# Exponentials and gate weights written in linear order, tokens kept by (parity, group, pair)

## The chip, the cores and the metric

The kernel runs on one core of a Trainium2 chip. The metric is device time in microseconds. Two runs of the kernel before took 212.56 and 213.94 us; their median, 213.25 us, is the time to compare with. The profiled execution took 212.8 us, and its span from the first to the last instruction is 211.1 us; all times within the profile count from the start of that span.

The engines are named as the profile names them: PE is TensorE (matmuls), PEld its weight loads, DVE is VectorE, ACT is ScalarE, POOL is GpSimd, SP is SyncE, which here only issues transfers.

## The reference

Attention with 32 memory slots instead of keys, and after it a mixture of experts. Batch B = 8, heads H = 8, sequence S = 576, head size 64, memory slots M = 32, experts E = 8, D = F = 512.

```python
def _attn_ref(q, k, v, phi):
    a = np.exp(phi - np.max(phi, axis=2, keepdims=True))
    a = a / (np.sum(a, axis=2, keepdims=True) + 1e-09)
    k_m = np.einsum('bhsm,bhsd->bhmd', a, k)
    v_m = np.einsum('bhsm,bhsd->bhmd', a, v)
    scores = np.matmul(q, k_m.transpose(0, 1, 3, 2)) / np.sqrt(q.shape[-1])
    attn = np.exp(scores - np.max(scores, axis=-1, keepdims=True))
    attn = attn / (np.sum(attn, axis=-1, keepdims=True) + 1e-09)
    return np.matmul(attn, v_m)
# x = the result as (4608 tokens, 512)
def _moe_ref(x, w_gate, w1_dense, w2_dense, w1, w2):
    y_dense = np.maximum(x @ w1_dense, 0.0) @ w2_dense
    logits = x @ w_gate
    expert_idx = np.argmax(logits, axis=1)
    probs = softmax(logits)                      # cut
    gate_w = probs[np.arange(N), expert_idx]
    # each token: one expert e = expert_idx
    y_moe = gate_w * (np.maximum(x @ w1[e], 0.0) @ w2[e])
    return y_dense + y_moe
```

## The kernel before

The eight batches go through a software pipeline whose order of steps is written out by hand, one list for all engines. A step name and its batch stand in it, such as `s:4` (scores of batch 4), `ET0:4` (its first exponentials), `Z0:4`, `ln0:4`, `inv0:4`, `A0:4` (the normalised weights), `hd0:4` (first layer of the dense part), `yd0:4` (second layer), `he`, `ye` the same for the expert that most tokens of the batch choose, `o0:4` a store. Within one engine the instructions run in that order. The change keeps the list.

Inputs lie in SBUF with 64 groups of nine consecutive tokens: partition p of a head holds tokens 9p to 9p + 8. So the scores come out with columns (t, p), t from 0 to 8 the place in the group, p the group, first the five even t, then the four odd ones. The columns that leave the exponentials are put into token order, 9p + t, by the way they are written. Cut to what the change touches:

```python
P = 64; T = S // P                                # T = 9
NP = S // 256; NCH = 2 * NP + 1; REM = S - 256 * NP   # 2, 5, 64
cols = [slice(256 * (c // 2) + c % 2, 256 * (c // 2) + 256, 2) for c in range(2 * NP)]
cols.append(slice(S - 128, S))
rem = slice(S - REM, S)
even, odd = slice(0, P * (T - T // 2)), slice(P * (T - T // 2), S)

big = ctx.enter_context(tc.tile_pool(name="big", bufs=2, space=PSUM))   # p_q, p_kv, p_s, p_z, p_h
one = ctx.enter_context(tc.tile_pool(name="one", bufs=3, space=PSUM))   # p_vw, p_y

# s: scores of both halves of a batch, a = 0 and 1, each in one tile of "big"
for a in range(2):
    p_s = big.tile([128, 2, 512], F32, tag="big", name="p_s")
    st[b]["ps", a] = split(p_s)                   # 576 of the 1024 columns
...
# ET0, ET1: exponentials of half a
p_s = st[b].pop(("ps", a))
for u, cs in enumerate((even, odd)):
    nc.scalar.activation(
        out=st[b]["ET"][:, a].rearrange("m (p t) -> m t p", t=T)[:, u::2],
        in_=p_s[:, cs].rearrange("m (t p) -> m t p", p=P),
        func=AF.Exp, scale=escale)
...
# Z: sums over the 32 slots, by a matmul with blocks of ones; ln, inv: 1/sum = exp(-ln(sum))
# A: ET * inv, f16
# second layer, columns of tokens as lhsT
def second(b, c, HT, w2):
    p_y = one.tile([128, 512], F32, tag="one", name="p_y")
    at, n, parts = (rem, REM, 2) if c == NCH - 1 else (cols[c], 128, 1)
    ...
            nc.tensor.matmul(p_y[n * u : n * u + n, 0:w], lhsT=HT[:, ft, at],
                             rhs=w2[:, ft, w * u : w * u + w], ...)
# the gate logits use the same columns of A as lhsT
# o0, o1: 256 rows; o4: the last 64 rows in two halves
nc.sync.dma_start(
    out=out[S * b + 256 * c : S * b + 256 * c + 256].rearrange("(p i) d -> p (i d)", i=2),
    in_=st[b]["y"][:, 2 * D * c : 2 * D * c + 2 * D])
# wgt: the gate weights, once, at the start
o = wgt[:, i].rearrange("t e p -> t p e")
r = st[0]["wgr"][:, i].rearrange("t (p e) -> t p e", e=E)
copy(e, out=o, in_=r)                             # on ScalarE
# w1: the expert's weights; GpSimd waits for the number of the expert (choose), then issues
# w1, w2 of this batch and loads of later batches that stand behind them in its queue
```

Of the kernel before, what the change touches and what calls it, by code (L numbers as in the profile page):

```python
# [13 lines left out]
AF = mybir.ActivationFunctionType  # L14
# [53 lines left out]
def kernel(  # L68
# [13 lines left out]
    nc = tc.nc  # L82

    B, H, S, Dh = q.shape
    M = phi.shape[-1]
    D = out.shape[1]
    E = moe_w_gate.shape[1]
    F = moe_w1_dense.shape[1]
    P = 64
    T = S // P  # L90
# [3 lines left out]
    NJ = H // 2  # L94
    SC = 16.0
    escale = 1.0 / (math.sqrt(Dh) * SC)
    NP = S // 256
    NCH = 2 * NP + 1
    REM = S - 256 * NP
    cols = [slice(256 * (c // 2) + c % 2, 256 * (c // 2) + 256, 2) for c in range(2 * NP)]  # L100
    cols.append(slice(S - 128, S))
    rem = slice(S - REM, S)
    even, odd = slice(0, P * (T - T // 2)), slice(P * (T - T // 2), S)
    NKEEP = 4

    const = ctx.enter_context(tc.tile_pool(name="const", bufs=1))
# [10 lines left out]
    def copy(e, out, in_):  # L117
        (nc.scalar.copy if e == "A" else nc.vector.tensor_copy)(out=out, in_=in_)  # L118

    def split(p):  # L120
        return p.rearrange("p h c -> p (h c)")[:, 512 - even.stop : 512 - even.stop + S]

    order = ExitStack()
    order.enter_context(tc.manual_schedule())
# [22 lines left out]
    def step(*names):  # L147
        def reg(f):
            for n in names:
                steps[n] = f  # L150
            return f

        return reg

    st = [dict() for _ in range(B)]
# [15 lines left out]
    @step("Lphi")  # L171
    def _(b, i, e):
        input_tile(b, "phi")
        (nc.gpsimd if e == "P" else nc.sync).dma_start(
            out=st[b]["phi"].rearrange("p j t m -> p j (t m)"), in_=rows(phi[b])
        )
# [63 lines left out]
    def load_w1(out, e, cond=None):  # L240
        nc.gpsimd.dma_start(  # L241
            out=out, in_=moe_w1[ds(e, 1)].rearrange("o (dt p) f -> p (o dt) f", p=128), cond=cond
        )

    def load_w2(out, e, cond=None):
        nc.gpsimd.dma_start(
            out=out, in_=moe_w2[ds(e, 1)].rearrange("o (ft p) d -> p (o ft) d", p=128), cond=cond
        )
# [31 lines left out]
    @step("wgt")  # L280
    def _(b, i, e):
        wgt = wk.tile([DT, 2, E, 64], F16, tag="qT", name="wgt")
        st[0]["wgt"] = wgt
        for i in range(2):
            o = wgt[:, i].rearrange("t e p -> t p e")
            r = st[0]["wgr"][:, i].rearrange("t (p e) -> t p e", e=E)
            if e == "P":
                nc.gpsimd.tensor_copy(out=o, in_=r)
            else:
                copy(e, out=o, in_=r)  # L290
# [175 lines left out]
    @step("ET0", "ET1")  # L466
    def _(b, a, e):
        if "ET" not in st[b]:
            st[b]["ET"] = wk.tile([128, 2, S], F16, tag="ET", name="ET")
        p_s = st[b].pop(("ps", a))  # L470
        for u, cs in enumerate((even, odd)):
            nc.scalar.activation(  # L472
                out=st[b]["ET"][:, a].rearrange("m (p t) -> m t p", t=T)[:, u::2],
                in_=p_s[:, cs].rearrange("m (t p) -> m t p", p=P),
                func=AF.Exp,
                scale=escale,
            )

    @step("Z0", "Z1")
    def _(b, a, e):  # L480
# [297 lines left out]

    @step(*(f"o{c}" for c in range(NP)))
    def _(b, c, e):  # L780
        nc.sync.dma_start(
            out=out[S * b + 256 * c : S * b + 256 * c + 256].rearrange("(p i) d -> p (i d)", i=2),
            in_=st[b]["y"][:, 2 * D * c : 2 * D * c + 2 * D],
        )

    @step(f"o{NCH - 1}")
    def _(b, c, e):
        y = st[b]["y"][:, 2 * D * NP :]
        dst = out[S * b + S - REM : S * b + S]
        w = D // 2  # L790
        for u in range(2):
            eng = nc.scalar if u == 1 and e == "A" else nc.sync
            eng.dma_start(out=dst[:, w * u : w * u + w], in_=y[REM * u : REM * u + REM, 0:w])
# [30 lines left out]
    def go(text):  # L824
        for tok in text.split():
            tok, _, e = tok.partition("/")
            name, _, b = tok.partition(":")
            if name in ("kv", "kk", "vv", "kvm", "kmk", "kmv", "T", "Tk", "Tv"):
                steps[name](int(b), name, e)
                continue  # L830
            i = name if name[0] in "LFC" and name[1:2] in ("k", "v", "q") else int(name[-1]) if name[-1].isdigit() else 0
            steps[name](int(b), i, e)
# [4 lines left out]
    def others(b):  # L837
        st[b].clear()
        go(
            f"Lphi:{b}/P Lk:{b} Lv:{b} Lq:{b} e0:{b} e1:{b} z:{b} rz:{b} kv:{b} kvm:{b} T:{b} kTc:{b}/V"  # L840
            f" q0:{b} qT0:{b}/V q1:{b} qT1:{b}/V s:{b} ET0:{b} ET1:{b} Z0:{b} ln0:{b} Z1:{b} ln1:{b}"
            f" inv0:{b} inv1:{b} A0:{b} A1:{b}"
        )
        ix = sm.tile([128, NCH], F32, tag="ix", name="ix")
        nc.vector.tensor_scalar(
            out=ix,
            in0=idx[b],
            scalar1=em[:, b : b + 1],
            scalar2=100.0,
            op0=ALU.is_equal,  # L850
            op1=ALU.mult,
        )
        nc.vector.tensor_add(out=ix, in0=ix, in1=idx[b])
        y0 = wk.tile([128, 2 * NP, D], F32, tag="y", name="yx", bufs=NKEEP)
        y1 = wk.tile([128, D], F32, tag="lnz", name="yr")
        y = [y0[:, c] for c in range(2 * NP)] + [y1]
        rows_of = [
            (y0[:, 2 * c : 2 * c + 2].rearrange("p i d -> p (i d)"), S * b + 256 * c)
            for c in range(NP)
        ]  # L860
        for t, r in rows_of:
            nc.gpsimd.dma_start(
                out=t, in_=out[r : r + 256].rearrange("(p i) d -> p (i d)", i=2)
            )
        tail = out[S * b + S - REM : S * b + S]
        nc.gpsimd.dma_start(out=y1[128 - REM :], in_=tail)
        for e in range(E):
            w1e = wk.tile([128, DT, F], F16, tag="HTd", name="w1x")
            w2e = wk.tile([128, FT, D], F16, tag="qT", name="w2x")
            load_w1(w1e, e)  # L870
            load_w2(w2e, e)
            ge = sm.tile([128, NCH], F32, tag="ge", name="ge")
            nc.vector.scalar_tensor_tensor(
                out=ge,
                in0=ix,
                scalar=float(e - E),
                in1=gate[b],
                op0=ALU.is_equal,
                op1=ALU.mult,
            )  # L880
            nc.vector.tensor_scalar(
                out=ge, in0=ge, scalar1=1.0 / SC, scalar2=None, op0=ALU.mult
            )
            HTx = wk.tile([128, FT, S], F16, tag="HTe", name="HTx")
            vwx = wk.tile([128, 2, F], F16, tag="vwe", name="vwx")
            for a, p_vw in enumerate(fold(vT[b], w1e)):
                nc.vector.tensor_copy(out=vwx[:, a], in_=p_vw[:, 0:F])
            for ft in range(FT):
                nc.vector.tensor_scalar_max(
                    out=HTx[:, ft].rearrange("p (h c) -> p h c", h=2),  # L890
                    in0=hidden(vwx, st[b]["A"], ft)[:, :, 0:HC],
                    scalar1=0.0,
                )
            for c in range(NCH):
                skip = 128 - REM if c == NCH - 1 else 0
                p_y = one.tile([128, 512], F32, tag="one", name="p_y")
                for ft in range(FT):
                    nc.tensor.matmul(
                        p_y,
                        lhsT=HTx[:, ft, cols[c]],  # L900
                        rhs=w2e[:, ft],
                        start=(ft == 0),
                        stop=(ft == FT - 1),
                    )
                nc.vector.scalar_tensor_tensor(
                    out=y[c][skip:],
                    in0=p_y[skip:],
                    scalar=ge[skip:, c : c + 1],
                    in1=y[c][skip:],
                    op0=ALU.mult,  # L910
                    op1=ALU.add,
                )
        for t, r in rows_of:
            nc.gpsimd.dma_start(
                out=out[r : r + 256].rearrange("(p i) d -> p (i d)", i=2), in_=t
            )
        nc.gpsimd.dma_start(out=tail, in_=y1[128 - REM :])

    engs = (ENG.PE, ENG.DVE, ENG.Activation, ENG.Pool)
# [36 lines left out]
```

The softmax here doesn't subtract the row's maximum and nothing guards it: scores larger than these inputs give would overflow.

## Time and profile before

| | |
|---|---|
| time, median of 2 runs | 213.25 us (212.56 to 213.94) |
| span of the profiled execution | 211.1 us, 5096 instructions |
| TensorE busy | 152.9 us (72%), mean granted clock 0.913 |
| ScalarE busy | 133.6 us (63%) |
| VectorE busy | 111.7 us (53%) |
| GpSimd busy | 35.5 us (17%) |
| bytes moved by transfers | 39.34 MB, 186 GB/s over the span; HBM read 51.92 MB, written 9.44 MB |
| chain that ended last | PE 53%, ACT 26%, DMA 11% of the span |
| its largest lines | PE p_y L741 27%, ACT ET L472 20%, PE p_h L677 15%, DMA fq 7%, DMA phi 5% |

A busy share is an average over the whole span and does not tell which engine holds up which. The chain that ended last is followed back from the last instruction: at each step to what released it. The view of stages gives, for any window of time, how long each engine was busy in it, at which clock TensorE ran, and what the DMA engines did. L472 is the exponential of the scores (ET), L677 the first layer (p_h), L741 the second (p_y), L483 the sums (p_z).

The loads from HBM cast f32 to f16 on the way, apart from those of the first batch, and phi. Until about 18 us the first batch waits for its inputs; after the last matmul, at about 201.8 us, the last stores land.

### The profile page before, as it was taken

What the parts mean: (1) busy time and instruction counts of PE and PEld (TensorE: products, weight loads), DVE (VectorE), ACT (ScalarE), POOL (GpSimd) and SP (SyncE); (2) the same over time, 40 slices, a digit from 0 to 9 for tenths busy, and PEclk for the clock granted to TensorE, in tenths of its full rate; (3) what the DMA queues carried; (4) which work ended last, traced back from release to release, by engine and by line L of the source; (5) the groups of instructions that cost most, each with busy time, mean ns of one, the idle gap of its engine ahead of it and who ended that gap; (6) DMA issues with size and microseconds to landing.
All of it is one profiled execution on the core that took longest, in us unless ns stands there. A gap on an engine that the chain in (4) does not pass through costs nothing.

```text
span 211.1 us, 5096 instructions
## 1 busy us (share of the span) xinstructions
PE 152.9 (72%) x2145; PEld 85.9 (41%) x2145; DVE 111.7 (53%) x289; ACT 133.6 (63%) x184; POOL 35.5 (17%) x53
## 2 busy tenths in 40 slices
PE   0034339829995999769759993999499947999920
PEld 0033116415652565336335641554246623556410
DVE  0324147425964686648826863466509553684630
ACT  2743884397749874798786378586867486545400
POOL 7400008000604500060003505200002000200000
PEclk9999999976999999999988997599769995899995
DMA  5999975995399999939991999999502994868460
GB/s 172 265 287 263 217 123 85 206 261 101 48 247 219 200 257 250 189 55 205 207 276 30 185 269 207 208 263 240 180 3 18 189 382 161 121 136 292 199 231 8
DMA packets 28149, 39.34 MB, mean 186 GB/s; under 512 B 1364, under 2 KB 24404, under 8 KB 28120
## 3 DMA queue, kind: packets, MB, share of 16 engines
q0 software_dynamic: 21840, 25.37, 68.3%
q1 hardware_dynamic: 6200, 13.52, 18.3%
q8 instruction: 18, 0.29, 0.5%
q14 instruction: 11, 0.09, 0.1%
q10 hardware_dynamic: 80, 0.07, 0.1%
HBM read 51.92 MB, written 9.44 MB: 291 GB/s over the span
## 4 chain that ended last, share of the span: by engine, by line
PE 53%; ACT 26%; DMA 11%; DVE 2%; issue 2%; SPq 1%; DVEq 0%; ACTq 0%
PE p_y L741 27%; ACT ET L472 20%; PE p_h L677 15%; DMA fq<-in_q_dram 7%; DMA phi<-in_phi_dram 5%; PE p_q L432 2%; PE p_kv L362 2%; PE p_z L483 2%; PE p_s L458 2%; PE p_att L611 1%; ACT E L329 1%; ACT lnz L496 1%; ACT lnz L505 1%; ACT HTd L717 1%; DVE qT L118 1%
## 5 line engine op out<-in xcount | busy, mean ns | idle before, releaser
L472 ACT ACTIVATE ET<-p_s 128x320 f16<-128x320 f32 (+1 forms) x32 | 42.0, 1689 | 4.4 <-PE p_s L458 4.3
L741 PE MATMUL p_y<-w2d,HTd 128*128 128x512 f16 (+1 forms) x192 | 42.2, 382 | 0.4 <-ACT vwe L118 0.2
L741 PE MATMUL p_y<-W,HTe 128*128 128x512 f16 (+1 forms) x192 | 36.4, 346 | 0.0
L775 DVE SCALAR_TENSOR_TENSOR y<-p_y,gm,y 128x512 f32<-128x512 f32 (+1 forms) x40 | 27.1, 692 | 7.9 <-PE p_y L741 6.1
L677 PE MATMUL p_h<-A,vwe 128*128 128x288 f16 x128 | 24.5, 331 | 7.9 <-ACT ET L472 7.7
L241 POOL DMA_DIRECT2D W<-in_moe_w_dram x8 | 6.0, 746 | 143.7 <-issue 64.4
L677 PE MATMUL p_h<-A,vwd 128*128 128x288 f16 x128 | 22.2, 308 | 8.5 <-ACT ET L472 5.8
L717 ACT ACTIVATE HTd<-p_h 128x576 f16<-128x576 f32 x26 | 17.1, 675 | 16.5 <-PE p_h L677 16.5
L741 PEld LDWEIGHTS <-HTd 128*128 128x128 f16 (+1 forms) x192 | 16.4, 112 | 14.9 <-issue 5.1
L766 ACT ACTIVATE y<-p_y 128x512 f32<-128x512 f32 (+1 forms) x24 | 13.8, 583 | 12.9 <-PE p_y L741 12.6
L677 PEld LDWEIGHTS <-vwe 128*128 128x128 f16 x128 | 13.5, 110 | 17.6 <-issue 11.6
L719 DVE TENSOR_SCALAR HTe<-p_h 128x576 f16<-128x576 f32 x14 | 10.5, 757 | 17.5 <-PE p_h L677 15.6
L741 PEld LDWEIGHTS <-HTe 128*128 128x128 f16 (+1 forms) x192 | 14.4, 102 | 12.9 <-issue 2.0
L677 PEld LDWEIGHTS <-vwd 128*128 128x128 f16 x128 | 12.2, 103 | 15.6 <-issue 6.8
L483 PE MATMUL p_z<-ET,blk 128*128 128x288 f16 x32 | 8.8, 375 | 12.9 <-ACT ET L472 12.9
L717 ACT ACTIVATE HTe<-p_h 128x576 f16<-128x576 f32 x18 | 11.7, 668 | 8.4 <-PE p_h L677 8.2
L496 ACT ACTIVATE lnz<-p_z 128x576 f32<-128x576 f32 x16 | 10.8, 688 | 6.4 <-PE p_z L483 6.3
L512 DVE TENSOR_TENSOR A<-ET,lnz 128x576 f16<-128x576 f16 x16 | 11.8, 753 | 5.0 <-ACT lnz L505 4.9
L768 DVE TENSOR_SCALAR y<-p_y 128x512 f32<-128x512 f32 (+1 forms) x16 | 9.7, 606 | 8.1 <-PE p_y L741 7.6
L118 DVE COPY qT<-p_q 128x1152 f16<-128x1152 f16 x8 | 6.0, 753 | 15.0 <-PE p_q L432 15.0
L118 DVE CAST vwd<-p_vw 128x512 f16<-128x512 f32 x14 | 9.2, 681 | 8.8 <-PE p_vw L664 8.7
L329 ACT ACTIVATE E<-phi 128x576 f16<-128x576 f32 x16 | 11.4, 719 | 2.0 <-DMA phi<-in_phi_dram 2.0
(86 smaller groups left out, 185.2 us busy)
## 6 DMA issues: line engine op xcount, KB each, us to landing
W<-in_moe_w_dram POOLq DMA_DIRECT2D x16, 512.0 KB, 7.4
out_dram<-y SPq DMA_DIRECT2D x16, 512.0 KB, 3.6
kv<-in_v_dram POOLq DMA_DIRECT2D x8, 576.0 KB, 13.9
q<-in_q_dram POOLq DMA_DIRECT2D x7, 576.0 KB, 7.9
kv<-in_k_dram POOLq DMA_DIRECT2D x7, 576.0 KB, 16.5
phi<-in_phi_dram POOLq DMA_DIRECT2D x5, 576.0 KB, 10.4
fk<-in_k_dram SPq DMA_DIRECT2D x2, 576.0 KB, 5.9
fq<-in_q_dram SPq DMA_DIRECT2D x2, 576.0 KB, 12.9
```

The source lines that it names most:

```text
L118: (nc.scalar.copy if e == "A" else nc.vector.tensor_copy)(out=out, in_=in_)
L329: nc.scalar.activation(out=x["E"][:, :, hs].rearrange("p t j m -> p j t m"), in_=x["phi"][:, hs], func=AF.Exp,)
L472: nc.scalar.activation(out=st[b]["ET"][:, a].rearrange("m (p t) -> m t p", t=T)[:, u::2], in_=p_s[:, cs].rearrange("m (t p) -> m t p", p=P ...
L483: nc.tensor.matmul(p_z[:, h, 0:HC], lhsT=blk, rhs=st[b]["ET"][:, a, HC * h : HC * h + HC], start=True, stop=True,)
L496: nc.scalar.activation(out=st[b]["lnz"][:, a].rearrange("p (h c) -> p h c", h=2), in_=st[b].pop(("pz", a))[:, :, 0:HC], func=AF.Ln,)
L512: eng.tensor_mul(out=st[b]["A"][:, a], in0=st[b]["ET"][:, a], in1=st[b]["lnz"][:, a])
L677: nc.tensor.matmul(p_h[:, h, 0:HC], lhsT=vw[:, g, 128 * ft : 128 * ft + 128], rhs=a[:, g, HC * h : HC * h + HC], start=(g == 0), stop=(g = ...
L717: nc.scalar.activation(out=o, in_=in_[:, :, 0:HC], func=AF.Relu)
L719: nc.vector.tensor_scalar_max(out=o, in0=in_[:, :, 0:HC], scalar1=0.0)
L741: nc.tensor.matmul(p_y[n * u : n * u + n, 0:w], lhsT=HT[:, ft, at], rhs=w2[:, ft, w * u : w * u + w], start=(ft == 0), stop=(ft == FT - 1),)
L766: nc.scalar.activation(out=o, in_=p_y, func=AF.Copy, scale=1.0 / SC)
L775: nc.vector.scalar_tensor_tensor(out=o, in0=p_y, scalar=x["gm"][:, c : c + 1], in1=o, op0=ALU.mult, op1=ALU.add)
```

## The change

The exponentials are written side by side, and the token columns keep the order that results: parity u of the place in the group, then the group p, then the pair k (places t = 2k + u, t from 0 to 7). The ninth tokens of all groups stand at the end, 64 columns. So in each half one instruction covers 512 columns and reads the scores with a stride, where before two, of 320 and 256 columns, read them in order and wrote them with a stride; a second one copies the order of the 64 ninth tokens. The chunks of 128 columns for the second layer and the gate become contiguous: chunk (h, u) has the tokens of 32 groups and one parity. Two chunks of a store, u = 0 and 1, hold pairs of neighbouring rows, so a store has 32 groups of 4 row pairs with a gap after each group, and the ninth tokens go out as rows 9 apart. The gate weights' copy is turned in the same way: it reads with a stride and writes in order. The aim is to take strided writes off ScalarE. No instruction is added or removed on any engine, and the order of the steps is the same. A fallback path that did not run on this input gets the same addresses.

```diff
-    NP = S // 256
+    K2 = T // 2
+    NP = P * K2 // 128
     NCH = 2 * NP + 1
     REM = S - 256 * NP
-    cols = [slice(256 * (c // 2) + c % 2, 256 * (c // 2) + 256, 2) for c in range(2 * NP)]
+    cols = [slice(P * K2 * u + 128 * h, P * K2 * u + 128 * h + 128) for h in range(NP) for u in range(2)]
     cols.append(slice(S - 128, S))
     rem = slice(S - REM, S)
-    even, odd = slice(0, P * (T - T // 2)), slice(P * (T - T // 2), S)
+    even, odd = slice(0, P * (T - K2)), slice(P * (T - K2), S)
@@
     def split(p):
-        return p.rearrange("p h c -> p (h c)")[:, 512 - even.stop : 512 - even.stop + S]
+        at = 512 - even.stop
+        return p.rearrange("p h c -> p (h c)")[:, at : at + 2 * even.stop]
+
+    def tokens(b):
+        return out[S * b : S * b + S].rearrange("(p t) d -> p t d", t=T)
+
+    def rows_out(b, h):
+        n = P // NP
+        o = tokens(b)[n * h : n * h + n, 0 : 2 * K2]
+        return o.rearrange("p (k u) d -> p k (u d)", u=2)
@@ wgt
-            o = wgt[:, i].rearrange("t e p -> t p e")
-            r = st[0]["wgr"][:, i].rearrange("t (p e) -> t p e", e=E)
+            o = wgt[:, i]
+            r = st[0]["wgr"][:, i].rearrange("t (p e) -> t e p", e=E)
@@ ET0, ET1
-        p_s = st[b].pop(("ps", a))
-        for u, cs in enumerate((even, odd)):
-            nc.scalar.activation(
-                out=st[b]["ET"][:, a].rearrange("m (p t) -> m t p", t=T)[:, u::2],
-                in_=p_s[:, cs].rearrange("m (t p) -> m t p", p=P),
-                func=AF.Exp,
-                scale=escale,
-            )
+        p_s, ET = st[b].pop(("ps", a)), st[b]["ET"][:, a]
+        nc.scalar.activation(
+            out=ET[:, 0 : 2 * P * K2].rearrange("m (u p k) -> m u p k", u=2, k=K2),
+            in_=p_s.rearrange("m (u k p) -> m u p k", u=2, p=P)[:, :, :, 0:K2],
+            func=AF.Exp,
+            scale=escale,
+        )
+        nc.scalar.activation(
+            out=ET[:, rem], in_=p_s[:, even.stop - REM : even.stop], func=AF.Exp, scale=escale
+        )
@@ o0, o1
         nc.sync.dma_start(
-            out=out[S * b + 256 * c : S * b + 256 * c + 256].rearrange("(p i) d -> p (i d)", i=2),
-            in_=st[b]["y"][:, 2 * D * c : 2 * D * c + 2 * D],
+            out=rows_out(b, c), in_=st[b]["y"][:, 2 * D * c : 2 * D * c + 2 * D]
         )
@@ o4
-        dst = out[S * b + S - REM : S * b + S]
+        dst = tokens(b)[:, T - 1]
(cut: the same in the fallback path)
```

More of the change, by code (lines that the diff above doesn't have):

```diff
@@ L857, in others @@
         rows_of = [
-            (y0[:, 2 * c : 2 * c + 2].rearrange("p i d -> p (i d)"), S * b + 256 * c)
+            (y0[:, 2 * c : 2 * c + 2].rearrange("p i d -> p (i d)"), rows_out(b, c))
             for c in range(NP)
@@ L861, in others @@
         for t, r in rows_of:
[L862 to L865, printed above, removed]
+            nc.gpsimd.dma_start(out=t, in_=r)
+        tail = tokens(b)[:, T - 1]
         nc.gpsimd.dma_start(out=y1[128 - REM :], in_=tail)
@@ L913, in others @@
         for t, r in rows_of:
-            nc.gpsimd.dma_start(
-                out=out[r : r + 256].rearrange("(p i) d -> p (i d)", i=2), in_=t
-            )
+            nc.gpsimd.dma_start(out=r, in_=t)
         nc.gpsimd.dma_start(out=tail, in_=y1[128 - REM :])
```

## The prediction

> **What bounds the kernel now.** I read the page's table of instruction groups first, for the group that the diff rewrites, then the chain that ended last, then the waits, and last the stages, in windows of time laid over the eight batches. In the groups by form the columns are instructions, busy time and mean of one in ns, then idle time before them and its releaser:
>
> ```profile
> L472 ACT ACTIVATE ET<-p_s 128x320 f16<-128x320 f32 x16 | 28.0, 1751 | 4.4 <-PE p_s L458 4.3
> L472 ACT ACTIVATE ET<-p_s 128x256 f16<-128x256 f32 x16 | 26.0, 1627 | 0.0
> L717 ACT ACTIVATE HTd<-p_h 128x576 f16<-128x576 f32 x26 | 17.1, 675 | 16.5 <-PE p_h L677 16.5
> ...
> L329 ACT ACTIVATE E<-phi 128x576 f16<-128x576 f32 x16 | 11.4, 719 | 2.0 <-DMA phi<-in_phi_dram 2.0
> ```
>
> An exponential of 320 or 256 columns takes 1.6 to 1.75 us, while ScalarE does 576 columns of the same types in 0.68 us when it writes them side by side. The exponential over phi (0.72 us) shows that the function is not the reason; its output is written in runs of 32 values. What sets L472 apart is the destination: successive values land 9 f16 values, 18 bytes, apart. By the page the 32 of them fill 42.0 us, two pairs per batch, 5.25 us a batch.
>
> Do they lie on the path? The waits say yes, and the chain says how:
>
> ```profile
> PE p_h L677 <- ACT ET L472: 13.5, 8, 2.5
> PE p_z L483 <- ACT ET L472: 12.9, 8, 2.7
> ```
>
> ```profile
> 146.11 5.26 ACT ET L472 x4
> ...
> 151.41 2.08 PE p_h L677 x8
> ...
> 158.92 0.98 PE p_h L677 x8
> ```
>
> In these waits (total, times, longest) TensorE stands still 26.4 us, twice in each batch. The score tiles p_s of a batch fill both buffers of the "big" PSUM pool, so no p_h, p_z or p_q can be opened until the first pair of exponentials has emptied one. The chain (start, length) counts 19.6% of the span, 41.4 us, for L472. It also shows a second loss: right after the exponentials eight p_h matmuls take 2.08 us, and a few microseconds later eight of them take 0.98.
>
> The stages show both. Columns are window, length, busy TensorE with its instructions, granted clock, share of the DMA engines, GB/s; first the eight stretches of exponentials, then the work between some of them:
>
> ```profile
> 21.70:26.90 5.20, 1.24 (x16) 1.00 1.23 212
> 42.20:47.40 5.20, 1.43 (x22) 0.72 1.17 262
> 63.00:68.20 5.20, 2.57 (x14) 1.00 1.18 232
> 87.50:92.80 5.30, 3.25 (x27) 1.00 0.44 75
> 103.10:108.40 5.30, 1.99 (x22) 1.00 1.08 284
> 125.10:130.40 5.30, 1.85 (x20) 0.94 1.22 213
> 146.10:151.40 5.30, 2.00 (x20) 0.90 0.93 273
> 170.20:175.40 5.20, 1.24 (x24) 0.88 0.95 369
> ```
>
> ```profile
> 69.00:86.00 17.00, 16.84 (x242) 1.00 1.18 235
> ...
> 109.00:124.00 15.00, 15.00 (x208) 0.89 0.80 157
> 131.00:145.00 14.00, 14.00 (x196) 0.80 1.21 229
> 152.00:169.00 17.00, 17.00 (x218) 0.85 0.44 67
> ```
>
> Between exponentials TensorE is busy all the time; within them it works 15.6 of 42.0 us. So the kernel is TensorE's, with eight holes of some 3.3 us, and the holes are ScalarE's. After the holes of batches 1, 4, 5, 6 and 7 the clock is at half: over 47.4 to 49.3, 130.4 to 134.6, 151.4 to 155.1 and 175.4 to 179.0 us it is 0.50, and 0.70 over 108.4 to 110.7. TensorE is busy 15.5 us there; weighted by clock that is 8.2 us of full-speed work, so 7.3 us go to the slow clock.
>
> **What the Trainium skill says.** "Advanced Engine Details and Errata", section "Memory Cachelines": SBUF lines are 16 bytes, and an access pattern that goes to another line with each element pays for it; PSUM lines are 8 bytes. The trace agrees for the write, where each value is on another line: 1.31 us per instruction (5.25 over four) for 288 columns on average, 4.5 ns a column, against 675/576 = 1.2 ns. How ScalarE fares on a strided PSUM read, the new side of the trade, is on no row of this trace. "ScalarE: Activation LUTs", section "What ACT_TABLE_LOAD costs", gives 186 ns plus 0.833 ns a column with immediate scale and bias, 666 ns for 576; the trace has 668 to 688. "TensorE: Matmul & The Clock Gate", "Part 1: The HAM clock gate", says that TensorE falls to half clock after a window of some 3.4 us without enough work and recovers after one busy window. The trace agrees in kind: each of the five slow stretches lies behind such a hole, and lasts a few microseconds. "DMA: Bandwidth & Descriptors", section "Why a DMA increments its semaphore by 16 and not by 1", lets the slowest dimension choose the number of engines; 32 groups still divide by 16. No run here has shown that form of store.
>
> **The change part by part.** (1) Exponentials. A pair goes from 320 + 256 columns with strided writes to 512 + 64 with linear ones. For 512 columns into f16 ScalarE's copies of p_vw take 567 to 586 ns; for 64 I estimate 220 ns, between the 203 of 40 columns (L634) and the 267 of 128. Back to back instructions overlap by about 0.1 us (two E of 0.68 take 1.26). A pair is then 0.70 us, a batch 1.4 instead of 5.25, ScalarE 42.0 - 11 = 31 us less. TensorE's gain is bounded by what it waited, 26.4 us. The matmuls it has at hand during the exponentials (1.2 to 3.3 us a batch) cover most of 1.4 us, but the first p_h still needs the first pair done; I leave 0.3 us a batch, 2.4 in all. On the path: 24.0 us less. In batch 0, where the chain runs through ScalarE, the saving is 5.25 - 1.4 = 3.85, about the 3.96 that TensorE idles there, so the same count holds.
>
> (2) Clock. With holes of under half a microsecond most of the half-clock stretches should go. Each batch keeps a run of small matmuls (p_kv, turning, scores) around the exponentials, so I count a little over half of the 7.3 us: 4.0.
>
> (3) Gate weights. Two copies of 2.62 us become some 0.6 each, around 6.4 to 11.2 us. ScalarE then waits for phi (0.55 us) and twice for fq (4.1 us), and the first scores come after fq. Zero.
>
> (4) Token columns. The lhsT of the second layer and of the gate logits now lies side by side instead of every other column. Weight loads of strided HTd and HTe take 107 and 98 ns, of contiguous vwd and vwe 103 and 110; they are hidden behind matmuls. Zero.
>
> (5) Stores. As many descriptors as before, 128 rows of 4 KB each, and 1 KB pieces for the ninth tokens, with gaps in HBM instead of one run. Only the last ones show, about 9 us after the final matmul. Zero.
>
> (6) Given back. The DMA engines are full for long: from about 54 to 89 us, and 114 to 149, at about 205 GB/s landed as f16, from twice as many bytes of f32 in HBM. The critical chain has 9.83 us of phi for batch 4 in the first of them. By then the compute wants to run ahead by 3.9 + 3.3 + 2.6 = 9.8 us, but this stretch can only start earlier by the first two and 0.9 of clock, some 7 to 8. I take 3 us for it and for the W loads of batches 1 and 4, which land only some 2 to 4 us ahead of use. Another 2.5 us for new waits: the instruction order is fixed by hand and fits the old durations.
>
> Sum: 24.0 + 4.0 - 3.0 - 2.5 = 22.5 us. 213.25 - 22.5 = 190.75; I say 190.5.
>
> **Rivals.** First, the stride only moves: the read of p_s now hops 256 bytes between the four values of a run. If it cost what the write cost, 512 columns would take 2.3 us and a batch 5.0, for a time of about 212. Against it: the new destination is the side on which the trace shows the price. At twice the linear rate a pair would be about 1.1 us, and the time 194. Second, the DMA becomes the bound. In the page's slices the saturated stretches up to 149 us add up to some 125 us, the rest are gaps while GpSimd waits to learn the chosen expert; these shrink with the compute. The last v and k land about 149 and are used at 167, 18 us ahead, so I expect local loss only; were DMA to hold the whole front, 197 to 200. Third, the slow clock stays, or denser work brings it on: 195. For: it came in five of eight batches. Against: over 69 to 86 us TensorE is busy 16.84 of 17 at clock 1.00. Fourth, all holes close and the clock holds: 26.4 + 7.3 off, 180.
>
> **Range and chances.** The middle of these is 188 to 195; the fourth rival sets the lower end, 182; a dear strided read with DMA waits the upper, 202. Only the stride merely moving leaves the time where it was, at about 4%, and nothing seen makes it slower: faster 0.95, within 2% 0.04, slower 0.01.
>
> **What would show it.** A 512-column group of exponentials at 0.58 us (0.9 or more: the read is dear) with a 64-column one near 0.22; TensorE's waits for ET under 4 us in total; mean clock above 0.93 instead of 0.913; more DMA waits for phi, kv and W around 50 to 85 us; stores of 512 KB still landing in about 3.6 us. I am wrong if ET keeps over 20 us of ScalarE, or if the waits on ET go and the span does not, with DMA names in their place.

## The result and the profile after

The changed kernel takes 177.19 us (176.64 and 177.73), against 213.25: 0.831 of the time before, with a 95% interval of 0.815 to 0.847. On record stood 190.5 us in a range of 182 to 202. The direction and the mechanism were as foretold; the time lies 4.8 us under the range. Two further sets of runs of both kernels gave 0.842 (0.834 to 0.851, e5) and 0.840 (0.834 to 0.845, e9).

The groups of ScalarE by form (instructions, busy us, mean ns, idle before), after:

```profile
L481 ACT ACTIVATE ET<-p_s 128x512 f16<-128x512 f32 x16 | 9.6, 601 | 4.5 <-PE p_s L468 4.5
L487 ACT ACTIVATE ET<-p_s 128x64 f16<-128x64 f32 x16 | 3.7, 232 | 0.0
...
L119 ACT CAST wgt<-wgr 4x512 f16<-4x512 f32 x2 | 2.1, 1103 | 4.2 <-DMA wgr<-in_moe_w_gate_dram 4.2
```

The exponential of 512 columns takes 601 ns although it reads PSUM with steps of 256 bytes; before, one of 320 took 1751. TensorE's waits for it (total, times, longest) have all but gone:

```profile
PE p_z L495 <- ACT ET L487: 1.2, 2, 0.7
...
PE p_h L689 <- ACT ET L487: 0.5, 1, 0.5
```

The chain that ended last (start, length), at the last batch, after:

```profile
139.37 0.48 PE p_s L468 x8
139.85 0.58 ACT ET L481
140.43 0.12 ACT ET L487
140.55 0.04 issue
140.59 0.65 PE p_h L689 x4
141.24 0.34 PE p_vw L676 x8
141.58 0.60 PE p_h L689 x4
```

Where ScalarE took 5.26 us on the chain, for all four exponentials of a batch, it takes 0.70, for the first pair alone, and the p_h behind it go at 0.60 to 0.65 per four, where before eight needed 2.08.

The stages, TensorE alone (window, length, busy and instructions, clock, DMA share, GB/s), first of the kernel before, from the first scores to the last matmul, then of the kernel after:

```profile
20.80:201.80 181.00, 148.49 (x1934) 0.92 0.89 185
```

```profile
20.70:165.50 144.80, 135.94 (x1934) 1.00 1.10 230
```

This is the whole account. What lies ahead of and behind this stretch has the same length in both, 30.1 us. Within it the kernel lost 36.2 us: TensorE is idle 8.9 us instead of 32.5, which is 23.6 of it, and busy 12.6 us less with the same 1934 instructions, at a clock of 1.00 instead of 0.92. The second part is three times the 4.0 us that I had set down for it. (Up to 34 us before and 30 us after, the clock column misleads; the last section shows how. TensorE is busy 6.6 us in that part of the stretch before and 6.0 after, so the 12.6 doesn't come from there.)

### The profile page after: what moved, and what is told of

The parts are those of the page before. It is cut to its first block, busy times and chain, and to the rows that moved or that the text cites. A ratio compares the mean times of both kernels' runs of the same rounds, so it can differ in the third digit from the quotient of the medians.

```text
span 174.9 us, 5096 instructions
## 1 busy us (share of the span) xinstructions
PE 140.3 (80%) x2145; PEld 81.2 (46%) x2145; DVE 111.5 (64%) x289; ACT 100.4 (57%) x184; POOL 35.5 (20%) x53
## 4 chain that ended last, share of the span: by engine, by line
PE 57%; DMA 20%; ACT 10%; DVE 4%; issue 3%; SPq 2%; POOLq 0%; ACTq 0%; DVEq 0%
PE p_y L753 30%; PE p_h L689 13%; DMA fq<-in_q_dram 8%; DMA phi<-in_phi_dram 6%; DMA W<-in_moe_w_dram 6%; PE p_z L495 2%; PE p_kv L372 2%; PE p_q L442 2%; PE p_vw L676 2%; ACT lnz L517 2%; PE p_s L468 1%; ACT lnz L508 1%; ACT HTd L729 1%; PE p_att L623 1%; ACT HTe L729 1%
## 5 line engine op out<-in xcount | busy, mean ns | idle before, releaser
L753 PE MATMUL p_y<-w2d,HTd 128*128 128x512 f16 (+1 forms) x192 | 37.3, 345 | 0.3 <-ACT vwe L119 0.2
L729 ACT ACTIVATE HTd<-p_h 128x576 f16<-128x576 f32 x26 | 16.4, 651 | 16.7 <-PE p_h L689 16.6
L689 PE MATMUL p_h<-A,vwd 128*128 128x288 f16 x128 | 21.2, 301 | 3.0 <-DVE cmx L562 2.5
L689 PE MATMUL p_h<-A,vwe 128*128 128x288 f16 x128 | 19.8, 285 | 0.9 <-ACT lnz L508 0.5
L753 PEld LDWEIGHTS <-HTd 128*128 128x128 f16 (+1 forms) x192 | 14.7, 101 | 12.0 <-issue 1.7
L778 ACT ACTIVATE y<-p_y 128x512 f32<-128x512 f32 (+1 forms) x24 | 13.3, 569 | 11.9 <-PE p_y L753 11.3
L689 PEld LDWEIGHTS <-vwe 128*128 128x128 f16 x128 | 11.7, 97 | 8.0 <-issue 3.0
L350 PE MATMUL p_att<-ones,E 128*128 128x2 f16 x72 | 3.0, 164 | 12.8 <-ACT E L339 12.8
L508 ACT ACTIVATE lnz<-p_z 128x576 f32<-128x576 f32 x16 | 10.2, 649 | 4.4 <-PE p_z L495 4.3
L481 ACT ACTIVATE ET<-p_s 128x512 f16<-128x512 f32 x16 | 9.6, 601 | 4.5 <-PE p_s L468 4.5
L517 ACT ACTIVATE lnz<-lnz 128x576 f32<-128x576 f32 x16 | 10.7, 683 | 0.3
```

The source lines that it names most:

```text
L481: nc.scalar.activation(out=ET[:, 0 : 2 * P * K2].rearrange("m (u p k) -> m u p k", u=2, k=K2), in_=p_s.rearrange("m (u k p) -> m u p k", u ...
L508: nc.scalar.activation(out=st[b]["lnz"][:, a].rearrange("p (h c) -> p h c", h=2), in_=st[b].pop(("pz", a))[:, :, 0:HC], func=AF.Ln,)
L517: nc.scalar.activation(out=lnz, in_=lnz, func=AF.Exp, scale=-1.0)
L689: nc.tensor.matmul(p_h[:, h, 0:HC], lhsT=vw[:, g, 128 * ft : 128 * ft + 128], rhs=a[:, g, HC * h : HC * h + HC], start=(g == 0), stop=(g = ...
L729: nc.scalar.activation(out=o, in_=in_[:, :, 0:HC], func=AF.Relu)
L778: nc.scalar.activation(out=o, in_=p_y, func=AF.Copy, scale=1.0 / SC)
```

## The experiments

All ran beside the kernel before, each set on one chip: e1 to e4, e5 to e8, e9 to e12. Ratios are to the kernel before of the same set. A run more than 1.5% above the fastest of its kernel counts as slow and is left out of the ratios, though not of the medians; that takes out 210.57 and 210.27 of e1, 180.27 of e8, 178.02 of e11 and three runs of the kernel before.

**e1: exponentials as long as before, in the new order.** Are the holes alone the cause, or do columns, stores and gate weights have a share?

```diff
-        nc.scalar.activation(out=ET[:, 0 : 2 * P * K2]..., in_=..., func=AF.Exp, scale=escale)
-        nc.scalar.activation(out=ET[:, rem], in_=..., func=AF.Exp, scale=escale)
+        for r in range(4):
+            nc.scalar.activation(out=ET[:, 0 : 2 * P * K2]..., in_=..., func=AF.Exp, scale=escale)
+            if r < 3:
+                nc.scalar.activation(out=ET[:, rem], in_=..., func=AF.Exp, scale=escale)
```

> The changed kernel with its exponentials written again into the same place: per half of a batch the instruction of 512 columns four times and that of 64 three times, 0.60 and 0.23 us each, which overlap to about 2.6 us, as long as the strided pair of the kernel before. Nothing else is changed. Theory (all of the gain is ScalarE's time in the eight holes, and the clock that follows from them): 211 to 216 us, TensorE waits on ET near 26 us again, mean clock 0.90 to 0.93. Rival (the order of token columns, stores and gate weights give a part of it, 5 us or more): 200 to 208 us with the same waits.

Measured: 210.22 us (207.10 to 210.57), ratio 0.983 (0.972 to 0.994), mean clock 0.918 in the profile. Its waits:

```profile
PE p_h L691 <- ACT ET L482: 12.4, 9, 2.3
PE p_z L497 <- ACT ET L482: 10.5, 7, 2.5
```

The time comes back almost whole. By the median it is 2.2 us below the 212.41 of its set, by the ratio 3.7 (1.3 to 6.0), and the waits are 3.5 us shorter than in the kernel before (22.9 against 26.4), because the repeats came out a little short: 4.86 us a batch instead of 5.25. The clock falls to half again with the holes of the same five batches, for 3.4 or 6.8 us each. The shorter waits leave the other parts between -2.2 and 2.5 us, as an estimate, and not the rival's 5, though one run of the four (207.10) lies in its span. The median lies 0.8 us under my span of 211 to 216, which the shorter waits cover.

**e2: the kernel before, with its holes filled.** Does the half clock follow from the holes, and what is it worth by itself?

```diff
+            # ahead of two waits in each of batches 1 to 7, N = 10 to 26:
+            p_x = one.tile([128, 512], F32, tag="one", name="p_x")
+            for _ in range(N):
+                nc.tensor.matmul(p_x[:, 0:128], lhsT=onesb, rhs=onesb, start=True, stop=True)
```

> The kernel before, with strided exponentials as they are, but with 10 to 26 matmuls without use (128 x 128 by 128 columns, into a buffer that nobody reads) just ahead of the two waits of each of batches 1 to 7: they fill some 60% of each wait. Theory (the half clock follows from idle holes): clock 0.97 or more, and 203 to 208 us, though the waits for ET stay. Rival (the half clock comes from something else, such as dense work): clock stays 0.90 to 0.92, and 213 to 216 us.

Measured: 205.9 us, ratio 0.971 (0.965 to 0.977), mean clock 0.99 in the profile. The page's totals, two groups, and the stage from the first exponentials on (window, length, busy TensorE, clock, DMA share, GB/s):

```profile
PE 154.5 (76%) x2365; PEld 94.0 (46%) x2365; DVE 111.8 (55%) x289; ACT 133.4 (66%) x184; POOL 35.6 (18%) x53
```

```profile
L474 ACT ACTIVATE ET<-p_s 128x320 f16<-128x320 f32 x16 | 28.1, 1758 | 4.6 <-PE p_s L460 4.5
...
L321 PE MATMUL p_x<-onesb 128*128 128x128 f16 x220 | 14.4, 219 | 3.3 <-DVE vwd L120 1.8 <-ACT y L768 1.0 <-DVE y L770 0.4
```

```profile
22.00:200.00 178.00, 149.67 (x2146) 1.00 0.91 190
```

The exponentials are as slow as ever, and 220 matmuls without use have been added, and the kernel is 6.5 us faster. Without the 14.4 us of fillers TensorE is busy 140.1 us, which is the changed kernel's 140.3: all of the drop in its busy time can be had with the clock alone. The gain is smaller than the 12.6 because the fillers also stand in the way: they take 14.4 us, and TensorE's idle time over the span falls by only 9.6 (58.2 to 48.6), partly because they wait for a buffer themselves (3.3 us).

**e3 and e6: no loads of expert weights.** Do the full DMA engines hold the changed kernel?

```diff
     @step("w1")
     def _(b, i, e):
+        if b:
+            return
@@ the same in w2; and in the steps that use them
-        st[b]["pve"] = fold(vT[b], W1[:, b])
+        st[b]["pve"] = fold(vT[b], W1[:, 0])
-        st[b]["pye", c] = second(b, c, st[b]["HTe"], W2[:, b])
+        st[b]["pye", c] = second(b, c, st[b]["HTe"], W2[:, 0])
```

This leaves out the other experts' results; all batches use the weights of batch 0.

> The changed kernel without the loads of the expert weights of batches 1 to 7 (14.7 of 51.9 MB read); all batches use the weights of batch 0, so the computing is left out for the other experts but the amount of work is the same. Theory (TensorE alone bounds the middle now, DMA only just keeps up): 174 to 177 us, less than 1.5% below the changed kernel's 177.2. Rival (the full DMA engines hold the kernel, as I had given back 3 us for): 165 to 171 us.

Measured: 180.45 us, ratio 0.851 (0.846 to 0.856). Neither theory had it slower than the changed kernel, so it ran again beside one, with this before it:

> The changed kernel once more, beside the others of this set, so that they can be compared on one chip: 176 to 179 us, 0.83 to 0.84 of the kernel before.

> The kernel of e3 again (no loads of expert weights for batches 1 to 7, so those experts' results are left out). It took 180.45 us there, 0.851 of the kernel before, which is more than the changed kernel's 0.831 and not less. Theory (TensorE bounds, and e3's 2% were the chip's): within 1% of e5. Rival (leaving loads out really costs, by a start or an end that shifts): 1.5 to 2% above e5.

Measured: e5 178.66 us, e6 180.41 us, ratio 0.849 (0.841 to 0.858), 1.0% above e5. So about half of e3's surplus is found again beside the changed kernel on one chip. In e6 the last work of VectorE, a cast of the flags, begins at 168.58 us, against 169.44 in e5, but its span ends at 178.5 against 177.1: what comes after the work is 2.3 us longer. In both traces the last packets to land are loads of instructions (176.7 us in e5, 177.2 in e6); why they come so long after the work in e6, the profile doesn't show. For the question it is enough: with 14.7 MB less to load the work is done 0.9 us sooner.

That answers for the part behind 80 us: over 110 to 140 us the share of the DMA engines is 0.12 in e6 and 1.20 in e5, but over 50 to 80 us they are as full in both, 1.18 and 1.19. For the part ahead of 80 us the stages above give a bound: between the first scores and the last matmul TensorE is idle 8.9 us in all, 6.9 of them ahead of 80 us, and transfers can't hold this stretch by more than that. So DMA hardly holds the changed kernel as a whole.

**e4: the price of a step.** Exponentials of 256 columns behind the end of the changed kernel, three of each.

```diff
+        act(d16[:, 0:n], lin)                                    # lin: PSUM, 256 columns
+        act(d16[:, 0:n] as (p 4), pb[:, 0:n] read as (4 p))      # read with a step of 256 bytes
+        for s in (2, 4, 8, 9, 16):
+            act(d16[:, 0 : s * n].rearrange("m (p t) -> m p t", t=s)[:, :, 0], lin)
+        act(pairs of d16 every 9 values, lin); act(pairs of d16 every 10 values, lin)
+        for s in (2, 9):
+            act(d32[:, 0 : s * n].rearrange("m (p t) -> m p t", t=s)[:, :, 0], lin)
+        act(d32[:, 0:n], s32[:, 0:n])
+        act(d16[:, 0:n], s32[:, 0 : 9 * n] read every 9 values)
```

> The changed kernel with exponentials of 256 columns added after its end, three of each kind: PSUM in order to SBUF f16 in order; read with a stride and written in order; written with steps of 4, 8, 16, 18 and 32 bytes; pairs of f16 every 18 and every 20 bytes; f32 written every 8 and every 36 bytes; SBUF f32 in order, and read every 36 bytes. Theory of 16-byte lines (price for each new line): 0.39 us in order, at 4 and 8 bytes still near 0.4, from 16 bytes on 1.2 to 1.5 us, f32 at 36 bytes as dear as f16 at 18. Rival (a write of 2 bytes alone costs, whatever the line, because memory takes 4 bytes at once): already 1.2 to 1.5 us at a step of 4 bytes, and f32 at 36 bytes near 0.4 us. Strided read from PSUM: 0.39 to 0.45 us by either.

The view of stages, ScalarE alone, one window for each kind in the order of the diff; the busy time is that of three (the two windows with x4 catch the end of the one before):

```profile
170.74:171.98 1.24, 1.15 (x3) 0.61 0.05 14
171.98:173.23 1.25, 1.15 (x3) 0.50 0.10 20
173.23:174.69 1.46, 1.37 (x3) 0.50 0.02 6
174.69:177.00 2.31, 2.21 (x3) 0.50 0.04 11
177.00:181.00 4.00, 3.91 (x3) 0.50 0.00 2
181.00:184.95 3.95, 3.86 (x3) 0.50 0.00 0
184.95:188.76 3.81, 3.71 (x3) 0.50 0.00 0
188.76:190.77 2.01, 1.91 (x3) 0.50 0.00 0
190.77:191.92 1.15, 1.06 (x3) 0.50 0.00 0
191.92:193.19 1.27, 1.19 (x4) 0.50 0.00 0
193.19:195.16 1.97, 1.87 (x3) 0.50 0.00 0
195.16:196.37 1.21, 1.13 (x3) 0.50 0.00 0
196.37:198.98 2.61, 1.97 (x4) 0.50 0.00 0
```

Mean of one instruction in each, from the trace:

```
from          to                         us
PSUM f32      SBUF f16, in order         0.384
PSUM, step 256 B read   f16, in order    0.384
PSUM f32      f16 every  4 B             0.455
PSUM f32      f16 every  8 B             0.737
PSUM f32      f16 every 16 B             1.302
PSUM f32      f16 every 18 B             1.287
PSUM f32      f16 every 32 B             1.238
PSUM f32      pairs of f16 every 18 B    0.637
PSUM f32      pairs of f16 every 20 B    0.398
PSUM f32      f32 every  8 B             0.391
PSUM f32      f32 every 36 B             0.624
SBUF f32      f32, in order              0.416
SBUF f32, every 36 B    f16, in order    0.649
```

Three things follow. The strided read of PSUM, with this step of 256 bytes, is free (first rival of the prediction: out). A strided write of single f16 values costs 3.5 ns each from 16 bytes on ((1.287 - 0.384)/256), and less the more of them share 16 bytes. But neither of my two theories is whole: f32 values at 36 bytes, each on its own line too, cost only 0.9 ns each, and f16 pairs every 20 bytes nothing to speak of, while pairs every 18 bytes, of which every other one straddles two 4-byte words, cost 0.25 us more than values in order. Dear is a word of four bytes of which only half is written, where it stands alone in its 16 bytes; four such words side by side in 16 bytes (a step of 4 bytes) add only 0.3 ns a value. That is a reading of these times, and not a whole one: it leaves open why single f32 values every 36 bytes cost 0.9 ns each and whole words of two f16 every 20 bytes nothing. Nor does the price carry over exactly: in the kernel before, 256 columns at the same step of 18 bytes took 1.627 us, 0.34 more than here, where no other engine was at work and the values came in one run and not in four of 64. Which of the two makes the difference isn't shown.

**e7: the old stores and gate weights.** Stores in one run of 256 rows and the ninth tokens as the last 64 rows, so that the rows land in another order; gate weights written with a stride.

```diff
-        o = tokens(b)[n * h : n * h + n, 0 : 2 * K2]
-        return o.rearrange("p (k u) d -> p k (u d)", u=2)
+        return out[S * b + 256 * h : S * b + 256 * h + 256].rearrange("(p i) d -> p (i d)", i=2)
-        dst = tokens(b)[:, T - 1]
+        dst = out[S * b + S - REM : S * b + S]
@@ wgt
-            o = wgt[:, i];  r = ....rearrange("t (p e) -> t e p", e=E)
+            o = wgt[:, i].rearrange("t e p -> t p e");  r = ....rearrange("t (p e) -> t p e", e=E)
```

> The changed kernel with the stores of the kernel before (256 rows in one run, ninth tokens as the last 64 rows, so rows land in another order) and the gate weights written with a stride again. Theory (both parts are worth nothing): within 0.5% of e5. Rival (32 groups with gaps in HBM store slower, or gate weights delay the start): 1% or more away from e5.

Measured: 178.1 us, 0.3% under e5, with runs that overlap (177.3 to 179.6, e5 178.4 to 179.4). The form of the store does show, off the path: issues of the changed kernel, then of e7 (KB each, median us to landing; 3.6 in the kernel before):

```profile
out_dram<-y SPq DMA_DIRECT2D x16, 512.0 KB, 4.7
```

```profile
out_dram<-y SPq DMA_DIRECT2D x16, 512.0 KB, 3.8
```

**e8: TensorE warmed at the start.** 70 fillers as in e2, between 11 and 26 us.

> The changed kernel with 70 matmuls without use (128 x 128 by 128 columns) in the idle stretches of TensorE between 11 and 26 us. The changed kernel's first eight p_h take 2.08 us and a later eight 0.98, so TensorE is at half clock there though the clock row says 1.00. Theory (the clock follows from what TensorE did just before): 2 to 3 us less than e5. Rival (the start is bound by inputs alone): no change, or up to 1 us more from fillers in the way.

Measured: 178.02 us, 0.4% under e5. Three runs (177.0 to 178.1) lie below all of e5, the fourth, 180.3, above: a gain of some 0.7 us, short of the 2 to 3. The p_h did come at full clock (eight in 1.14 us, busy, instead of 2.08), but the fillers were in the way of the first scores, which began 1.5 us later. In the profiled execution, the one of 180.3, the clock also fell to half once more, from 79.6 to 82.9 us. So the theory can't be read off this run; the next set separates the pieces.

**e9 to e12: the places where the changed kernel still waits.** e9 is the changed kernel. e10 gives phi a third buffer; e11 adds nine wide fillers; e12 puts GpSimd's copy of k, for which it must wait, ahead of its loads.

```diff
-            x["phi"] = inp.tile([128, NJ, T, M], F32, tag="phi8", name="phi8", bufs=2)
+            x["phi"] = inp.tile([128, NJ, T, M], F32, tag="phi8", name="phi8", bufs=3)
@@ e11: ahead of q0:0, Z1:0 and hd3:0, N = 2, 1 and 6
+            nc.tensor.matmul(p_x, lhsT=onesb, rhs=onesb.unsqueeze(1).to_broadcast([128, 4, 128]), ...)
@@ e12: order of steps
-Lv:0 cid:0 Fk1:0 Lphi0:0 Lw1d:0 Lq:1 Lw2d:0 Lv:1 ciota:0 Ck1:0/P ciotac:0
+Lv:0 cid:0 Fk1:0 Lphi0:0 ciota:0 Ck1:0/P Lw1d:0 Lq:1 Lw2d:0 Lv:1 ciotac:0
```

> The changed kernel once more as the measure for this set: 176 to 179 us.

> The changed kernel with three buffers for phi instead of two, so that the load of phi for batch 4 need not wait until the exponentials of batch 3 have read theirs (in the changed kernel ScalarE waits 3 us for it, and TensorE about 1 us behind that). Theory (TensorE bounds, DMA holds it in this one place by a microsecond or two): 1 to 2 us less than e9. Rival (the engines of the DMA are full there anyway, so an earlier issue lands no earlier): within 0.5 us of e9.

> As e10, and 9 matmuls without use of 512 columns ahead of the first batch's waits (2, 1 and 6), in place of e8's 70 narrow ones, which started the first scores 1.5 us late. Theory (the start is at half clock, and e8's gain was lost to its own fillers and to the wait for phi): 1 to 2 us less than e10. Rival (what the start gains, the DMA takes back later): within 0.5 us of e10.

> As e11, and GpSimd copies the first half of k before it issues the loads of the dense weights and of batch 1, so that these start about 4 us later and leave the DMA engines to q of batch 0, for which the first scores wait until 18 us. Theory (the first 20 us are bound by how loads share the engines): scores 2 to 3 us earlier and 1 to 3 us less than e11. Rival (bytes are bytes: what is put off is missed later): within 0.5 us of e11, or up to 2 us more.

| | us, median | single runs | ratio to before |
|---|---|---|---|
| e9 | 178.71 | 178.05 to 179.45 | 0.840 (0.834 to 0.845) |
| e10 | 176.98 | 176.75 to 177.33 | 0.832 (0.827 to 0.837) |
| e11 | 175.84 | 175.22 to 178.02 | 0.831 (0.821 to 0.840) |
| e12 | 174.45 | 174.04 to 175.55 | 0.822 (0.816 to 0.829) |

The exponentials over phi of batches 3 and 4 (start, length, idle before and releaser), in e9 and then in e10:

```profile
65.69 0.69 ACT L339 ACTIVATE E<-phi 128x576 f16<-128x576 f32 x1
77.00 0.68 ACT L339 ACTIVATE E<-phi 128x576 f16<-128x576 f32 x1 [2.16 <-DMA phi<-in_phi_dram]
```

```profile
66.19 0.69 ACT L339 ACTIVATE E<-phi 128x576 f16<-128x576 f32 x1
75.23 0.71 ACT L339 ACTIVATE E<-phi 128x576 f16<-128x576 f32 x1
```

With the third buffer ScalarE no longer waits there, and the kernel is 1.7 us faster, with no overlap of the runs. So the load of phi, which had waited for a free buffer, did hold the changed kernel, in this one place, by a little under 2 us. The fillers took another 1.1 us at the median. That is likely rather than certain: three runs (175.22 to 176.23) lie below all of e10 and one, 178.02, above, and the ratios, 0.832 and 0.831, don't tell the two apart. From the first exponentials of batch 0 to those of batch 1 it is 15.5 us instead of 17.0. e12's start brings the first exponentials to 20.5 us, from 21.7 in e11, so 1.2 us and not the 2 to 3 expected, and takes 1.4 us more at the median, with runs that overlap. e12 beats both kernels: 2.4% under e9, with no overlap.

## Why the prediction was off

**What bounds the kernel: right.** TensorE, with eight holes made by ScalarE's strided writes. e1 makes the holes again without the old layout and gets the time back.

**Step 1, the exponentials: right.** Foretold 0.58 and 0.22 us, measured 0.601 and 0.232; TensorE's waits foretold to fall by 24.0 us, and they fell by 24.7, from 26.4 to 1.7. This step makes 0.7 of the miss.

**Step 2, the clock: this is the one that failed, twice.** The mechanism was right (e2), but I sized the loss at 7.3 us and gave back only 4.0. The loss was some 12.8. I had laid windows from the end of each hole to a time at which I took the clock to have recovered, 49.3, 110.7, 134.6, 155.1 and 179.0 us, read 0.50 in most of them, and never asked whether the slow stretch went on. It did, by about two microseconds each time. The full stretches of the kernel before, where the clock goes down and comes up again:

```profile
44.50:51.30 6.80, 4.80 (x42) 0.50 0.98 171
109.30:112.70 3.40, 3.40 (x29) 0.50 0.80 144
129.80:136.60 6.80, 6.14 (x27) 0.50 1.23 209
150.30:157.10 6.80, 5.69 (x21) 0.50 0.05 14
174.20:181.00 6.80, 5.52 (x21) 0.50 0.46 125
```

The trace shows why it went on. All changes of the clock lie whole multiples of 3.41 us apart: the slow stretches last one or two such steps, the full-speed ones between them (58.0, 17.1, 13.7, 17.1 and, to the next fall, 23.9 us) 17, 5, 4, 5 and 7. In the step ahead of each of the five falls TensorE is busy 0.55 to 1.56 of the 3.41 us. The holes of batches 2 and 3 fall across two or three steps, with 1.66 to 2.82 us busy in each, and no fall follows. The step that ends a slow stretch has 3.15 to 3.41, a slow one that doesn't end it 1.65 to 2.76. So in this trace a hole costs the clock or not by where it lies against the steps, and the price comes in whole steps. Busy time alone gives no sharp limit: a step of 1.66 us stayed fast here, one of 1.78 in e8 was followed by a fall.

TensorE is busy 25.55 us in the five slow stretches, so half of it, 12.8 us, is the price; the drop in its busy time is 12.6, and e2 finds the same. That the windows were too short could be seen: one gave 0.70, a window that mixed two states, and a window that gives exactly 0.50 shows only that it lies inside a slow stretch, not where that ends. The second half of the mistake was to expect the stretches to stay for half: the small matmuls around the scores, which I gave as reason, don't lower the clock in the changed kernel; it stands at 1.00 from 30 us to the last matmul. Of the 13.3 us between 190.5 and 177.2, this step makes 8.6 (12.6 - 4.0).

**Steps 3 to 5, gate weights, columns, stores: right, nothing.** e1 bounds the three together to some 2 us and e7 the first and the last to about 1. The gate weights' copy fell to 1.10 us and not 0.6; its read from SBUF has a step of 32 bytes, and e4 has the same kind of read at 0.65 instead of 0.42 us. TensorE's waits don't name it. The stores land 0.9 us later than in e7, which the end doesn't feel: from the last matmul it takes 9.4 us, before 9.3.

**Step 6, what is given back: 5.5 us expected, 1.1 found.** TensorE's idle time fell by 23.6 us where its waits for the exponentials fell by 24.7, so 1.1 us of other waits came on top. The largest of them is the wait of the first p_vw for ScalarE, which had itself waited for phi of batch 4; it grew from 0.6 to 1.0 us. I was right on the place, phi of batch 4, and e10 gives its worth as 1.7 us. I was wrong that saved compute runs into the DMA engines much further: their share went from 0.89 to 1.10 over the middle stretch without holding it further. This step makes 4.4 of the 13.3 us. (The three terms add up to 13.7, as the two profiles differ by a little more than the medians and I had rounded the sum down.) The waits that I feared from an order of steps made for the old durations stayed within this 1.1 us.

**The rivals.** The fourth, all holes closed and the clock held, was what happened; at 180 it too rested on the 7.3 us, and with 12.8 in its place the same sum gives 174. The lower end of the range was built on it and fell with it. The stride didn't just move (e4), the DMA isn't the bound (e3, e6 and TensorE's 8.9 us of idle time), and the slow clock, the third rival, neither stayed nor came with denser work.

Of the Trainium skill, "TensorE: Matmul & The Clock Gate", "Part 1: The HAM clock gate", was borne out where it mattered: its window of some 3.4 us is the step of the clock here, the slow stretches are 6.8 and 3.4 us long, and filling the idle ahead of them removed them. But no window had to be idle throughout: TensorE's longest single wait in those holes was 2.5 us. "Advanced Engine Details and Errata", section "Memory Cachelines", holds for the write in its direction, but by e4 the word of 4 bytes counts too, beside the line of 16, and the small lines of PSUM cost ScalarE's read nothing.

## What to carry to other kernels

When one engine makes TensorE wait, the price is the wait and, where the clock falls, the slow stretch behind it, and here the second was half of the first; take the slow stretch from where the clock goes down to where it comes up, and count half of the busy time inside. If a value must be permuted on its way from PSUM to SBUF, let ScalarE read with the stride and write in order (seen here for a step of 256 bytes), or, by one measurement of e4, write f16 in aligned pairs. When matmuls without use make a kernel faster, as in e2, the holes are worth closing properly.

## What the runs showed that I had not expected

- f16 written singly every 16 bytes or more: 1.24 to 1.30 us for 256 columns, 3.4 times the 0.384 in order; f32 every 36 bytes 0.624; aligned pairs of f16 every 20 bytes 0.398.
- A read of PSUM by ScalarE with a step of 256 bytes costs the same 0.384 us as one in order, but a read of SBUF every 36 bytes 0.649 against 0.416.
- The clock column shows 1.00 from the start of the kernel, while the first eight p_h take 2.08 us in both kernels, twice the 0.98 of later ones. Each p_h lasts 0.45 us until 34.1 us in the kernel before and 29.7 in the changed one, and 0.29 right after. So for the start of these traces the column can't be relied on, and batch 0 ran slow in both.
- Leaving out 14.7 MB of loads finished the work 0.9 us sooner and the program 1.8 us later, by a longer end. Why the end grew stays open.
